# Local attention in 48-query blocks on four 64x64 tiles, global keys in three groups, and part of q and k transposed by DMA

## The chip, the cores and the metric

The kernel runs on one core of a Trainium2 chip. The metric is the device time of one execution in microseconds (us). Runs of the kernel before took 363.45, 364.85 and 365.05 us; the median is 364.85.

The engines are named as the profile names them: PE is TensorE's matmul stream and PEld its weight loads, DVE is VectorE, ACT is ScalarE, POOL is GpSimd, SP is SyncE, which here only issues transfers. A trailing q (SPq) is an engine's queue of instructions.

## The reference, cut to what matters

An attention layer (8 batches, 8 heads, 576 tokens, 64 numbers per head) is followed by an expert layer of two matrix products with ELU between them. The attention is the sum of two softmax attentions: a local one, in which a query sees the keys less than 4 tokens away, and a global one over means of four consecutive tokens (144 queries, 144 keys), whose output is repeated four times.

```python
q_d = q.reshape(B, H, Sd, factor, D).mean(axis=3)      # factor = 4, Sd = 144
k_d = k.reshape(B, H, Sd, factor, D).mean(axis=3)
v_d = v.reshape(B, H, Sd, factor, D).mean(axis=3)
out_d = sm_attn(q_d, k_d, v_d)
out_up = np.repeat(out_d, factor, axis=2)
mask = np.abs(pos[:, None] - pos[None, :]) < factor
scores = np.where(mask, scale * np.matmul(q, k.transpose(0, 1, 3, 2)), -1e9)
out_local = np.matmul(softmax(scores), v)
x = (out_up + out_local)                               # to 4608 tokens x 512
h = x @ w_in                                           # 512 x 2048
g = np.where(h > 0.0, h, np.exp(np.minimum(h, 0.0)) - 1.0)
return g @ w_out                                       # 2048 x 512
```

## The kernel before

**The unit of attention** is a pair of heads of one batch: head e = 0 lies on partitions 0 to 63 and head e = 1 on 64 to 127 once q and k are turned (transposed so that the 64 numbers of a head run along the partitions). There are 4 pairs in each of 8 batches, 32 in all. The steps of a pair are:

- `load` (L433 on): SP loads q and k of the pair as float32, 96 partitions x 768 numbers. In batches 0 and 1 (`SIX`) a partition holds six consecutive tokens (rows of 1536 bytes, L442); in the others a partition takes one token from each of six blocks of 96 tokens (rows of 256 bytes, L444).
- `cast` (L507 on): GpSimd (VectorE for q of batch 0) casts them to float16 tiles `c16`, L516.
- `transposes`: TensorE multiplies the cast tile by a constant. From batch 2 on there are six matmuls per tensor, whose 120 columns are a 96x96 identity and 24 columns that take the means of four (`ONE`, L548). In batches 0 and 1 there are twelve: six with an identity (L536) and six with `BY6`, which takes the means from the layout of six tokens per partition (L540). ACT (VectorE for k of batch 0) evicts the results into `qt`, `kt` and `KD` (L563 to L577).
- `scores`: twelve matmuls of 96 queries against 102 keys (L620), and four of 144 pooled queries against 102 rows of pooled keys (L628), in two groups `kg`. The contraction is over 64 numbers, so the two heads of a pair use the upper and the lower half of the array. Two exponentials on ACT (L637), one for each head, and one multiplication by the band mask on VectorE (L644) follow.
- `denominators`, once per batch (twice for batch 0): 72 small matmuls with indicator columns (L665) collect the sums of the exponentials of four pairs in one bank, VectorE takes the reciprocals (L692, 144 columns). From batch 2 on they are spread over the partitions by a transfer to DRAM and back (`rd`, `rcb`, L719 and L724); in batches 0 and 1 (`BY_PE`) by matmuls with `SEL` (L707) and an eviction (L714).
- `pool_v`: pooled v of a batch, 6 matmuls of 512 columns (L591), in the same TensorE operation as the denominators from batch 1 on; two evictions (L604).
- `outputs`: 12 matmuls with v (L748) and 8 with pooled v (L756) per pair, the two heads side by side in the columns of the array. `normalize` multiplies by the reciprocals on VectorE (L771), then adds the repeated global part to the local one on GpSimd (some of batch 0 on VectorE, L787), into `xt`.

v is loaded by SP as blocks of 96 tokens with their neighbours, 112 rows (L470), and cast by GpSimd (L473).

**The expert layer** works on 9 blocks of 512 tokens. `mm1` makes 16 groups of 4 matmuls of 128x512 per block (L804); ACT takes the exponential (L810), VectorE a minimum and a sum (L812) and the combination into `gt` (L815). `mm2` makes 16 groups of 4 matmuls per block (L827), ACT evicts `os` (L842) and SP stores it (L845). That is 1152 matmuls of 512 columns.

**The order of everything** is made by `Plan.run` when the program is built. It is a list scheduler: each operation has an engine, a planned duration, a rank (its due time, worked out from `PARAM`) and buffers from small pools (`SLOTS`). At each moment an engine takes the operation of the lowest rank whose inputs and buffers are there in the planner's own time; the order that comes out is fixed in the program. On the chip each engine, and each queue of transfers, goes through its list in order and waits where an input is late. `fill` (L329) puts matmuls on zeros between the real ones at the beginning. All loads of q, k and v and all stores of the result are issued by SP, so they stand in one queue in the planned order.

Of the kernel before, what the change touches and what calls it, by code (L numbers as in the profile page):

```python
# [18 lines left out]
NB, QB = 6, 96  # L19
KW = QB + 6  # L20
VB = 112
HB = 3 * QB
HD = SD // 2
GW = HB + HD
# [5 lines left out]
SIX = (0, 1)  # L30
EARLY = 1
DEN_GROUPS = {0: ((0, 1), (2, 3))}
# [4 lines left out]
BY_PE = (0, 1)  # L37
# [4 lines left out]
def _np_sel():  # L42
    sel = np.zeros((NPAIR, 32, 5, 2, 64), dtype=np.float16)
    for e in range(2):
        for i in range(5):
            sel[:, 5 * e + i, i, e] = 1.0
    return sel.reshape(128, 640)
# [22 lines left out]
class Plan:  # L70
# [24 lines left out]
    PARTS = ("v16", "v32", "rcb", "xt", "gt", "ex")  # L95
# [158 lines left out]
    def emit(self):  # L254
        for o in self.order:
# [4 lines left out]
    "ld": 8, "c16": 4, "v16": 2, "v32": 1, "qt": 3, "kt": 3, "ex": 8, "vd": 2,  # L260
# [3 lines left out]
PARAM = dict(M0=30, P=36.77, LAG=1.06, LEAD=53.49, GAP=7.69, SC=3.9, DEN=33.04, OUT=1.4, OUTG=1.98,  # L264
             LOAD=23.14, VLOAD=27.91, VCAST=36.99, warm=3.4, FILL=27.63, WI=-27.58, WO=38.12, WOG=2.24,
             OVER=1.0, LEAD1=57.82, GAP1=5.57, OUT1=32, VLOAD1=41.43, LOAD1=28.31, CC=-45.43, tv0=-26.96,
             C0=-7.99, SC0=2.71, OUTA=-25.9, OUTB=-21.42, DEN0=3.42, DENB=-28.86, SPA=-26.1, SPB=-20.87,
             V0=-46.5, G0=1, G1=2, G2=3, G3=3, G4=3, G5=8, G6=3, G7=13, G8=13, L0=2, L1=6, L2=0, L3=8,
             L4=0, LAG0=1.07, QG=2.08)
# [3 lines left out]
def kernel(  # L273
# [15 lines left out]
    def many(kind, shape, dt=FP16):  # L289
        return [sb.tile(shape, dt, tag=f"{kind}{i}", name=f"{kind}_{i}") for i in range(SLOTS[kind])]  # L290

    T = {
        "ld": many("ld", [QB, 2, NB, 64], FP32),
        "c16": many("c16", [QB, NB, 2, 64]),
        "v16": many("v16", [KW, NPAIR, 2, NB, 64]),
        "v32": many("v32", [115, 48, 64], FP32),
        "qt": many("qt", [128, 720]),
        "kt": many("kt", [128, S + 6]),
        "ex": many("ex", [KW, 2, 2, HB + SD]),
        "vd": many("vd", [QB, 2, NPAIR, 128]),  # L300
        "rcb": many("rcb", [128, NPAIR, 2, GW]),
        "rc": many("rc", [128, SD]),
        "xn": many("xn", [128, 2, GW]),
        "xt": many("xt", [128, DMC, TBLK]),
        "gt": many("gt", [128, FCN, TBLK]),
        "e": many("e", [128, TBLK]),
# [622 lines left out]
```

## Time and profile before

| what | value |
|---|---|
| runs of the kernel | 363.45, 364.85, 365.05 us |
| span of the profiled execution | 362.9 us, granted TensorE clock 0.984 |
| first matmul of the expert layer (L804) | at 37.56 us |
| matmuls of the expert layer | 576 (L804) and 576 (L827) |
| matmuls that transpose, batches 2 to 7 (L548) | 288 |
| ACT: exponentials of the scores (L637) | 64, mean 887 ns |
| VectorE: mask (L644) | 32, mean 895 ns |
| VectorE: minimum (L812) | 144, mean 386 ns |
| GpSimd: casts of q and k (L516) | 60, mean 861 ns |
| transfers on SP's and ACT's hardware queues | 108038 packets, 39.49 MB |
| a load of q, 288 KB, from issue to landing | 5.2 us (median) |

The profile is of one execution, whose span runs from its first to its last instruction. Matmuls are pipelined: the duration of one holds its way through the array, and the distance between the starts of two tells what one costs. In a timeline row stand the start in us, the time that the row's instructions cover, the engine, the source line, the operation, the tiles written and read, the shapes (for a matmul rows*columns of its weights, then partitions x columns of what streams through), the count, and in brackets the idle time of the engine before it with what ended it. In a list of waits stand who waited for whom, the sum in us, how often, and the longest.

### The profile page before, as it was taken

Reading aid. Unit: us, or ns where it says so; the run is one execution under the profiler, and the core shown is the slowest. Engines: PE = TensorE matmul, PEld = TensorE weight load, DVE = VectorE, ACT = ScalarE, POOL = GpSimd, SP = SyncE. Lnnn points to the kernel's source line nnn. Section 1 sums busy time; section 2 is a strip of 40 time slices with the busy share of each in tenths; the row PEclk is TensorE's granted clock in tenths of the full one; section 3 lists DMA queues with packets and bytes.
Section 4 is the critical chain, followed back from the end, with each engine's and each line's share of the span. In section 5 each row is a group of like instructions: output and inputs, shape, how many; then the busy total and the mean of one; then the engine's idle time right before and its main releaser. Section 6 shows DMA issues by size and latency. Waiting matters only on the chain.

```text
span 362.9 us, 8968 instructions
## 1 busy us (share of the span) xinstructions
PE 347.5 (96%) x3677; PEld 189.3 (52%) x3677; DVE 224.4 (62%) x410; ACT 211.5 (58%) x364; POOL 144.0 (40%) x226
## 2 busy tenths in 40 slices
PE   8995999999998998999999999999999999999995
PEld 7984554455454554554555455555554444444442
DVE  3658598336885597557755865398547667765510
ACT  2643696469865677557855785488557415544411
POOL 7645554277274544570557055634330160000000
PEclk9998799899999999999999999999999999999999
DMA  8999999999979799479746975103001311010021
GB/s 218 216 157 225 258 199 191 202 201 235 234 168 222 193 181 220 93 157 214 155 94 153 218 149 99 61 35 83 31 30 60 87 48 40 0 58 33 29 77 68
DMA packets 114366, 48.89 MB, mean 135 GB/s; under 512 B 100662, under 2 KB 108662, under 8 KB 114326
## 3 DMA queue, kind: packets, MB, share of 16 engines
q1 hardware_dynamic: 108038, 39.49, 52.3%
q0 software_dynamic: 6288, 8.84, 13.3%
q8 instruction: 28, 0.46, 0.6%
q14 instruction: 12, 0.10, 0.1%
HBM read 42.86 MB, written 9.66 MB: 145 GB/s over the span
## 4 chain that ended last, share of the span: by engine, by line
PE 78%; DVE 9%; ACT 6%; issue 2%; DMA 2%; POOL 2%; ACTq 0%; DVEq 0%; POOLq 0%
PE bank L827 32%; PE bank L804 27%; PE bank L548 4%; PE bank L620 3%; PE bank L748 3%; DVE e L812 3%; PE bank L329 3%; ACT e L810 2%; DVE gt L815 2%; PE bank L665 2%; ACT ex L637 2%; DVE ex L644 2%; DMA rcb<-rd 1%; PE bank L540 1%; PE bank L756 1%
## 5 line engine op out<-in xcount | busy, mean ns | idle before, releaser
L804 PE MATMUL bank<-xt,WI 128*128 128x512 f16 x576 | 141.2, 382 | 1.6 <-DVE gt L815 1.4
L827 PE MATMUL bank<-WO,gt 128*128 128x512 f16 x576 | 140.3, 381 | 1.9 <-DVE gt L815 1.9
L810 ACT ACTIVATE e<-bank 128x512 f16<-128x512 f32 x144 | 85.1, 603 | 49.1 <-PE bank L804 27.2
L815 DVE SCALAR_TENSOR_TENSOR gt<-bank,e 128x512 f16<-128x512 f32 x144 | 97.8, 688 | 4.9
L827 PEld LDWEIGHTS <-gt 128*128 128x128 f16 x576 | 54.0, 98 | 64.4 <-DVE gt L815 2.6
L804 PEld LDWEIGHTS <-WI 128*128 128x128 f16 x576 | 53.1, 98 | 64.0 <-issue 6.3
L812 DVE TENSOR_SCALAR e<-e 128x512 f16<-128x512 f16 x144 | 55.4, 386 | 39.6 <-ACT e L810 38.8
L516 POOL CAST c<-ld 96x768 f16<-96x768 f32 x60 | 50.6, 861 | 50.5 <-issue 25.7
L637 ACT ACTIVATE ex<-bank 102x864 f16<-102x864 f32 x64 | 53.4, 887 | 23.7 <-PE bank L628 23.5
L787 POOL TENSOR_TENSOR xt<-xn 128x288 f16<-128x288 f16 (+8 forms) x92 | 44.4, 514 | 54.1 <-DVE xn L771 54.0
L644 DVE TENSOR_TENSOR ex<-ex,MASK 102x1152 f16<-102x1152 f16 x32 | 28.6, 895 | 41.5 <-ACT ex L637 41.4
L842 ACT COPY os<-bank 128x512 f32<-128x512 f32 x36 | 21.3, 590 | 46.4 <-PE bank L827 43.4
L771 DVE TENSOR_TENSOR xn<-bank,rcb 128x720 f16<-128x720 f32 x32 | 27.8, 901 | 25.6 <-PE bank L756 23.8
L473 POOL CAST v<-v 102x768 f16<-102x768 f32 x32 | 27.5, 887 | 0.3 <-DMA v<-in_v_dram 0.3
L548 PEld LDWEIGHTS <-c 96*128 96x128 f16 x288 | 18.1, 97 | 8.0 <-issue 0.4
L563 ACT CAST qt<-bank 128x720 f16<-128x720 f32 x24 | 18.3, 761 | 4.2 <-PE bank L548 3.7
L548 PE MATMUL bank<-ONE,c 96*128 96x120 f16 x288 | 20.6, 216 | 0.0
L719 POOL DMA_DIRECT2D rd<-rc x6 | 3.5, 578 | 41.3 <-DVE rc L692 19.7
L329 PE MATMUL bank<-zero 128*128 128x128 f16 x221 | 17.3, 240 | 1.8 <-DVE ONE L355 1.1
L620 PEld LDWEIGHTS <-kt 64*102 64x102 f16 x384 | 11.7, 125 | 12.6 <-ACT e L810 4.7
L575 ACT CAST kt<-bank 128x576 f16<-128x576 f32 x24 | 15.6, 651 | 1.2 <-ACT qt L563 1.2
L329 PEld LDWEIGHTS <-zero 128*128 128x128 f16 x221 | 15.1, 109 | 2.4 <-DVE zero L332 1.1
(67 smaller groups left out, 228.6 us busy)
## 6 DMA issues: line engine op xcount, KB each, us to landing
ld<-in_q_dram SPq DMA_DIRECT2D x32, 288.0 KB, 5.2
ld<-in_k_dram SPq DMA_DIRECT2D x32, 288.0 KB, 5.4
out_dram<-os SPq DMA_DIRECT2D x36, 256.0 KB, 2.0
v<-in_v_dram SPq DMA_DIRECT2D x13, 672.0 KB, 8.8
rcb<-rd POOLq DMA_DIRECT2D x12, 360.0 KB, 5.6
WO<-in_moe_w_out_dram POOLq DMA_DIRECT2D x4, 512.0 KB, 9.1
WI<-in_moe_w_in_dram POOLq DMA_DIRECT2D x3, 512.0 KB, 11.3
v<-in_v_dram SPq DMA_DIRECT2D x3, 336.0 KB, 8.6
```

The source lines that it names most:

```text
L329: nc.tensor.matmul(PS[:, 7, 384:512], zero[:, 0:128], zero[:, 128:256], start=True, stop=True)
L516: f(out=at(y)[:], in_=at(x)[:].rearrange("p e c d -> p c e d"))
L548: nc.tensor.matmul(o, t[:, c, :, :], C["ONE"][:], start=True, stop=True)
L637: lambda e=e: nc.scalar.activation(out=at(x)[:, e], in_=two(sc[e], 0, KW, 0, HB + SD), func=AF.Exp, scale=SCALE),
L644: nc.vector.tensor_tensor(out=a, in0=a, in1=mk, op=AB.mult)
L771: lambda: nc.vector.tensor_tensor(out=at(w)[:], in0=two(z, 0, 128, 0, GW), in1=at(y)[:, j], op=AB.mult),
L787: (nc.vector if eng == "DVE" else nc.gpsimd).tensor_tensor(out=at(xt(t))[:, j, o : o + n - a], in0=ln, in1=gn, op=AB.add)
L804: nc.tensor.matmul(one(h, 0, 128, 0, TBLK), WI[:, dc, 128 * fc : 128 * fc + 128], at(x)[:, dc, :], start=(dc == 0), stop=(dc == DMC - 1),)
L810: op("ACT", 0.55, r, lambda: nc.scalar.activation(out=at(e)[:], in_=one(h, 0, 128, 0, TBLK), func=AF.Exp), reads=[h], writes=[e], name=f"e ...
L812: op("DVE", 0.42, r, lambda: nc.vector.tensor_scalar(out=at(e)[:], in0=at(e)[:], scalar1=1.0, scalar2=-1.0, op0=AB.min, op1=AB.add), reads ...
L815: op("DVE", 0.64, r, lambda: nc.vector.scalar_tensor_tensor(out=at(gt)[:, fc, :], in0=one(h, 0, 128, 0, TBLK), scalar=0.0, op0=AB.max, in1 ...
L827: nc.tensor.matmul(one(z, 0, 128, 0, DM), at(gt)[:, fc, 128 * tt : 128 * tt + 128], WO[:, fc, :], start=(fc == 0), stop=(fc == FCN - 1),)
```

## The change

The local attention goes from 6 blocks of 96 queries and 102 keys to 12 blocks of 48 queries and 54 keys, on 64 partitions each. Even and odd blocks lie on the lower and upper 64 partitions of the scores, so a score matmul uses 64 rows (one head) and 64 columns (one parity) of the array, and four of these tiles fill it. The pooled keys come in three groups of 64 rows instead of two of 102. The tiles that hold exponentials, v and pooled v change accordingly, and the means are indexed in ten groups of 72 columns instead of five of 144 (`IND`, `GAP`, `SEL`).

All loads of q and k now use rows of six tokens. Two ways of turning them remain: `transposed` is the form that batches 0 and 1 had (twelve matmuls per tensor), and `turned` is a transfer that transposes the cast tile from SBUF to SBUF, issued by SP. `TURNED` picks q of batches 3 to 7 (`TQ` = 12 pairs in) and k of batches 4 to 7 (`TK` = 16): 36 of 64 tensors. Tensors of batch 2, and k of batch 3, that had six matmuls now have twelve. For turned tensors GpSimd forms the sums of four tokens in two steps (`pa`, one addition; `pb`, three), VectorE scales them (`pc`), and ACT copies a turned k into its padded layout (`kn`).

v is loaded in two halves of 64 partitions, each with its own transfer, and pooled v takes 24 matmuls of 256 columns in two operations of their own. The two exponentials per pair become one over 128 partitions, the mask covers half as many columns, the reciprocal 72 columns instead of 144. The multiplication in `normalize` is split in two instructions. `PARAM` holds other ranks throughout, so the planned order of all engines differs.

```diff
-SIX = (0, 1)
+NS, QB = 6, 48
+KB = 64
+LW = NS * QB
 SLOTS = {
-    "ld": 8, "c16": 4, "v16": 2, "v32": 1, "qt": 3, "kt": 3, "ex": 8, "vd": 2,
+    "ld": 8, "c16": 4, "sg": 3, "ex": 6, "v16": 2, "v32": 1, "ps": 1, "vd": 2,
...
+    TURNED = {(b, j, w) for b in range(2, B) for j in range(NPAIR) for w in "qk"
+              if NPAIR * b + j >= PARAM["TQ" if w == "q" else "TK"]}
...
-                if b in SIX:
-                    nc.sync.dma_start(out=t.rearrange("p e c d -> p e (c d)"), in_=sixes(src, b, j))
-                else:
-                    nc.sync.dma_start(out=t, in_=rows(src, b, j, 0, QB, 0, NB))
+                nc.sync.dma_start(out=at(x)[:].rearrange("p e c d -> p e (c d)"), in_=sixes(src, b, j))
...
-            nc.sync.dma_start(out=t[0:VB, c0:c1, :], in_=blocks(c0, c1, -3, VB))
+            nc.sync.dma_start(out=t[p : p + KB, c0:c1, :], in_=blocks(h, c0, c1, 0, KB))
...
+    def turned(b, j, i, y, w, r):
+        r += PARAM["TU"]
+        o = op("SP", 1.25, r + 0.1 * i,
+               lambda: nc.sync.dma_start_transpose(out=at(w)[:, i], in_=at(y)[:].rearrange("p c e d -> p (c e d)")),
+               reads=[y], writes=[w], nbytes=S * 256, rate=112e3, packet=36, name=f"tu{'qk'[i]}{b}{j}")
+
+        def natural():
+            nc.scalar.copy(out=KN[w.slot[0]][:, KOFF : KOFF + S], in_=at(w)[:, 1].rearrange("p c u -> p u c"))
+
+        if i:
+            op("ACT", 0.65, r + PARAM["KN"], natural, writes=[w], after=[o_fill, o], name=f"kn{b}{j}")
+
+    def pooled(b, j, dma, w, r):
+        u, a, n = Buf("ps"), dma[0], len(dma)
+
+        def first():
+            t = at(w)[:, a : a + n].rearrange("p w (c x) u -> p w c x u", x=2)
+            nc.gpsimd.tensor_tensor(out=at(u)[:, a : a + n], in0=t[:, :, :, 0], in1=t[:, :, :, 1], op=AB.add)
+
+        op("POOL", 0.15 + 0.5 * n, r + 1.0, first, after=[x for x in w.writers if x.name[:2] == "tu"], writes=[w, u], name=f"pa{b}{j}")
+
+        def second():
+            x = at(u)[:, a : a + n].rearrange("p w c (g u x) -> p w c g u x", g=6, x=2)
+            o = PD[w.slot[0]][:, a : a + n].rearrange("p w (g u) -> p w g u", g=6)
+            for m, (c0, x0, c1, x1) in enumerate(((0, 0, 1, 0), (2, 0, 0, 1), (1, 1, 2, 1))):
+                nc.gpsimd.tensor_tensor(out=o[:, :, :, m:24:3], in0=x[:, :, c0, :, :, x0], in1=x[:, :, c1, :, :, x1], op=AB.add)
+
+        o = op("POOL", 0.4 + 0.25 * n, r + 1.1, second, reads=[u], writes=[w], after=[o_fill], name=f"pb{b}{j}")
+
+        def scale():
+            t = PD[w.slot[0]][:, dma[-1]]
+            nc.vector.tensor_scalar_mul(out=t, in0=t, scalar1=1.0 / (16.0 if n == 2 else 4.0))
+
+        op("DVE", 0.13, r + 1.2, scale, writes=[w], after=[o], name=f"pc{b}{j}")
...
-            for g in range(2):
-                for i in range(3):
+            for s in range(3):
+                for x in range(4):
                     nc.tensor.matmul(
-                        PS[32 * i : 32 * i + 32, z.slot[0] + g, :], C["VR"][:], t[:, :, :, 3 * g + i, :],
-                        start=True, stop=True, tile_position=(0, 32 * i),
+                        PS[32 * x : 32 * x + 32, zs[g].slot[0] + s // 2, 256 * (s % 2) : 256 * (s % 2) + 256],
+                        C["VR"][:], t[:, 2 * g : 2 * g + 2, :, 2 * s + x % 2, :],
+                        start=True, stop=True, tile_position=(0, 32 * x),
                     )
...
-            for c in range(NB):
+            for c in range(2 * NS):
                 for e in range(2):
                     p = slice(64 * e, 64 * e + 64)
-                    qa = QB * c if m else 120 * c
                     nc.tensor.matmul(
-                        PS[0:KW, sc[e].slot[0] + c // 3, QB * (c % 3) : QB * (c % 3) + QB],
-                        kt[p, QB * c : QB * c + KW], qt[p, qa : qa + QB], start=True, stop=True,
+                        PS[64 * (c % 2) : 64 * (c % 2) + KB, z.slot[0] + e, QB * (c // 2) : QB * (c // 2) + QB],
+                        kn[p, QB * c : QB * c + KB], qt[p, :, 8 * c : 8 * c + 8].rearrange("p c u -> p u c"),
+                        start=True, stop=True,
                     )
+            for i in range(3):
+                for h in range(2):
+                    for e in range(2):
+                        p = slice(64 * e, 64 * e + 64)
+                        nc.tensor.matmul(
+                            PS[64 * h : 64 * h + 64, z.slot[0] + e, LW + GH * i : LW + GH * i + GH],
+                            pd[p, 1, 64 * i : 64 * i + 64], _free(pd[p, 0, 96 * h : 96 * h + 1], [[32, 3], [1, 24]]),
+                            start=True, stop=True,
+                        )
...
-        for e in range(2):
-            op("ACT", 0.84, r + 0.3 + 0.1 * e,
-               lambda e=e: nc.scalar.activation(
-                   out=at(x)[:, e], in_=two(sc[e], 0, KW, 0, HB + SD), func=AF.Exp, scale=SCALE),
-               reads=[sc[e]], writes=[x], name=f"ex{b}{j}{e}")
+        op("ACT", 1.07, r + 0.3, lambda: nc.scalar.activation(
+            out=at(x)[:], in_=two(z, 0, 128, 0, EW), func=AF.Exp, scale=SCALE), reads=[z], writes=[x], name=f"ex{b}{j}")
...
+            for s in range(NS):
+                for h in range(2):
                     for e in range(2):
                         nc.tensor.matmul(
+                            PS[64 * e : 64 * e + 64, z.slot[0] + h, QB * s : QB * s + QB],
+                            v_[64 * h : 64 * h + 64, j, e, s, :], ex[64 * h : 64 * h + 64, e, QB * s : QB * s + QB],
+                            start=True, stop=True,
                         )
+            for i in range(3):
+                for h in range(2):
+                    for e in range(2):
+                        o = 128 * (j % 2) + 64 * e
+                        nc.tensor.matmul(
+                            PS[64 * e : 64 * e + 64, z.slot[0] + h, LW:HW],
+                            d_[64 * h : 64 * h + 64, j // 2, i, o : o + 64],
+                            ex[64 * h : 64 * h + 64, e, LW + GH * i : LW + GH * i + GH],
+                            start=(i == 0), stop=(i == 2),
+                        )
```

Of `PARAM`, the prediction uses `TU` = -0.4 (the rank of a turning transfer) and `SC`, the rank of the scores, 3.9 before and 8.25 after, both counted from the same due time of the pair.

437 lines of the change are left out of this document (195 added, 242 removed).

## The prediction

> **What bounds the kernel now.** I read the page first, then TensorE's timeline over one batch in the middle, then the waits, then the timeline around the places where TensorE stood still.
>
> ```profile
> span 362.9 us, 8968 instructions
> PE 347.5 (96%) x3677; PEld 189.3 (52%) x3677; DVE 224.4 (62%) x410; ACT 211.5 (58%) x364; POOL 144.0 (40%) x226
> ```
>
> TensorE (PE) is busy nearly throughout, the others near half. A busy share says little of pipelined matmuls, so I price TensorE by slots: from the first start of an operation to the first start of the next. These are rows of TensorE's timeline between 132 and 149 us:
>
> ```profile
> 132.44 0.32 PE L665 MATMUL bank<-ex,GAP 96*32 96x72 f16 x16
> 132.57 0.44 PE L665 MATMUL bank<-ex,IND 102*32 102x144 f16 x20
> ...
> 132.96 0.62 PE L591 MATMUL bank<-v,VR 102*32 102x512 f16 x6
> 133.51 1.04 PE L804 MATMUL bank<-xt,WI 128*128 128x512 f16 x4
> ...
> 139.85 0.48 PE L620 MATMUL bank<-qt,kt 64*102 64x96 f16 x12
> 140.17 0.29 PE L628 MATMUL bank<-qt,kd 64*102 64x144 f16 x4
> 140.39 1.90 PE L804 MATMUL bank<-xt,WI 128*128 128x512 f16 x8
> 142.13 0.80 PE L548 MATMUL bank<-ONE,c 96*128 96x120 f16 x12
> 142.76 1.03 PE L804 MATMUL bank<-xt,WI 128*128 128x512 f16 x4
> ...
> 147.82 0.45 PE L748 MATMUL bank<-ex,v 102*64 102x96 f16 x12
> 148.10 0.30 PE L756 MATMUL bank<-ex,vd 96*64 96x72 f16 x8
> 148.24 0.42 PE L748 MATMUL bank<-ex,v 102*64 102x96 f16 x12
> ```
>
> Twelve transposing matmuls (L548) take 142.76 - 142.13 = 0.63 us, 52 ns each. A pair's scores take 0.54 us (139.85 to 140.39), about 0.44 in its 16 matmuls and 0.10 in leaving that array shape. A pair's output takes 0.42 (147.82 to 148.24). The expert layer's matmuls run at 0.216 us each: the page's 576 + 576 make 249 us, and from 291 us on they are nearly alone and nearly gapless. So the end is the sum of TensorE's slots, plus the start (the first L804 is at 37.56 us), plus its stalls. Over 0.216 us each, the dense matmuls lose about 12 us in all; about 5 are changes of shape, 7 are stalls. What makes a stall is seen here (all engines, 99 to 112 us):
>
> ```profile
> 99.82 1.60 POOL L473 CAST v<-v 102x768 f16<-102x768 f32 x2
> 100.19 1.38 DVE L812 TENSOR_SCALAR e<-e 128x512 f16<-128x512 f16 x1 [0.96 <-ACT e L810]
> 102.22 0.28 DVE L812 TENSOR_SCALAR e<-e 128x512 f16<-128x512 f16 x1
> ...
> 104.58 4.35 DVE L644 TENSOR_TENSOR ex<-ex,MASK 102x1152 f16<-102x1152 f16 x1 [0.43 <-ACT ex L637]
> 111.60 0.39 PE L827 MATMUL bank<-WO,gt 128*128 128x512 f16 x1 [1.29 <-DVE gt L815]
> ```
>
> L812 takes 0.28 us alone and 1.38 beside a GpSimd cast; the mask takes 4.35 where its median is 0.76, with GpSimd at work 3.97 us of it; TensorE then waits for VectorE's gt.
>
> **TensorE's part of the change.** *Turning.* A batch from 2 on now spends 48 matmuls at 52 ns, 2.5 us, on transposes. After, batches 4 to 7 spend none (-10.1). Batch 3 keeps k alone in the heavier form of batches 0 and 1 (12 matmuls per tensor; at 8.66 and 9.30 us two such groups follow each other 0.64 apart), so 4 x 0.63 = 2.5, unchanged. Batch 2 keeps q and k in that form, 8 x 0.63 = 5.0 (+2.5). Sum: -7.6 us.
>
> *Scores and outputs.* Each becomes 36 matmuls per pair (24 of 48 columns, 12 of 72) instead of 16 and 20. No row has four tiles split both ways, so the price per matmul is bounded: 16 GAP matmuls, four 32-column tiles at once, take 0.13 us, 8 ns each; the 8 of L756, 64-column weights two at a time, take 0.14 us, 17.5 each. 36 of them are 0.29 to 0.63 us. I take 14 ns, 0.50 us: nearer the L756 row because the weights are again 64 wide, and four tiles move 256 weight columns where GAP's four move 128. That is +0.06 on scores (0.44) and +0.08 on outputs (0.42), over the 28 pairs of batches 1 to 7 (batch 0 lies in the start): +1.7 and +2.2 us. By the bounds the two together range from -7.8 to +11.2.
>
> The Trainium skill speaks against this: TensorE: Matmul & The Clock Gate, Back-to-back issue gap and the floors before it, says that starts never come closer than about 25 ns however few columns. By it 36 matmuls would take 0.90 us and the two parts would cost +26 us instead of +3.9. The 16 GAP matmuls, at 8 ns each, contradict it where several tiles run side by side.
>
> *Denominators, pooled v, spreading.* 72 denominator matmuls become 56 (-0.3 us a batch by the GAP rate), pooled v goes from 6 of 512 columns three at a time (0.55 us) to 24 of 256 four at a time (six groups at half a dense 0.216, 0.65), now as two operations that may add a change of shape of 0.1 each. I take 0, bounds -2 to +2 over seven batches. Batch 1's spreading goes from 6 to 10 matmuls a pair: +0.4.
>
> TensorE in all: -7.6 + 1.7 + 2.2 + 0.4 = **-3.3 us**.
>
> **The other engines.** They set no end of their own but feed the stalls. ACT: two exponentials of 0.887 become one of 1008 columns; from 720, 864 and 576 columns (0.761, 0.887, 0.642) a column costs 0.83 ns, so 1.01: -0.76 x 32 = -24. Evictions of q and k (0.761 + 0.651 + 0.302 a pair, 24 pairs, 41 us) become about 22: eight pairs' worth of mixed evictions (7.5 + 3.7) and 16 copies of k at 0.65. VectorE: the mask halves (-11), reciprocals of 72 columns instead of 144 (-4), 20 small scalings (+3). GpSimd gains: a fp16 add costs 0.18 us + 1.75 ns a column (from 236 ns at 32 and 684 at 288), so the first sum of q and k is 1.19 us and the three second ones 3 x 0.35; for 16 pairs 2.2 each, for 4 pairs with q alone 1.5, **+42 us** on 144. That it stays off the path: in batches 4 to 7 it would be busy some 26 of 36 us. What it costs VectorE: L812 waits in 44 of 144 cases (606 ns mean against 289), the mask in 13 of 32, some 18 us lost for 144 of GpSimd, so 42 more cost 5 us, of which 7/18 reached TensorE: +2. Against that stand 43 us less on ACT and 12 on VectorE. I take stalls -1, bounds -4 to +5.
>
> **The start.** On the chain to the first L804 stand two denominator groups (36 and 25 matmuls shown, about 0.9 us each) and two reciprocals of 1.06; they lose about 1.4. SEL doubles (+160 KB) and v is read as 128 rows instead of 112 (+0.2 MB for batch 0): 0.36 MB at the 207 GB/s of the first 38 us is 1.7 us of transfers, hidden as long as they land before their readers. I take -0.5, bounds -2 to +2.
>
> **Transfers.** 36 transposing transfers, SBUF to SBUF, 144 KB each, are issued by SP between casts and scores. No row shows one. Lower bound of issue and landing: 0.31 and 2.2 us (a 288 KB load's issue; the 36 KB rd transfer's landing); upper: 2.7 and 8.8 (v). The loads of batches 2 to 7 move to 1536-byte rows, which can only relieve the queues. I take the loads' 5.2 us landing and cost it at 0, hidden by the lead that the code gives it: ranks put the transfer 0.4 us before and the scores 8.25 us after the same point.
>
> **Sum:** 362.9 - 3.3 - 0.5 - 1 = 358.1 us of span. The runs' median, 364.85, lies 1.95 over the profiled span, so **360 us**; by itself 354 to 364.
>
> **Rivals.** (1) *Four tiles truly at once.* If loading 256 weight columns costs no more than GAP's 128, scores and outputs fall to 0.30 us: 28 x 2 x 0.20 = 11 us less, 349. For it: the two column tiles of L756 do overlap. Against it: no row loads more than about 4 weight columns per ns (GAP 32/8.1, L756 64/17.5, L620 102/27).
>
> (2) *Slower: the transposing transfers come late.* Between a cast and the scores lie SP's issue (up to 2.7), the landing (2.2 to 8.8), GpSimd's sums (2.2) and up to two casts queued before them (1.7): with 5.2 for the landing 9.5 to 11.8 us, against the 8.65 of lead. SP's queue is in order and is mostly waiting already:
>
> ```profile
> SPq L845 <- ACT os L842: 169.0, 30, 20.1
> ```
>
> A transfer behind such a store can't run ahead, so lateness isn't paid once but at every pair, and TensorE, in order too, waits with all dense matmuls behind the scores. It decides from a landing of about 4 us on if issue and casts also queue; at 0.6 us for each of 20 pairs, +12: 372. Against it: the planned order leaves 8 us between pairs, and buffers for three pairs let a transfer start before it is due. Trainium skill, VectorE: DVE Perf Modes, The three transpose paths, gives 1309 ns for a DMA transpose of 128x128 against 390 on TensorE; six blocks would, by an estimate, take 7.9 us and fall on this rival's side. No run here shows it yet.
>
> (3) *GpSimd eats the gain.* All 5 us that VectorE loses reach TensorE, as after the 4.35 us mask: 365.
>
> **Chances.** The forecast 0.42, (1) 0.13, (2) 0.28, (3) 0.17. Range 350 to 371: it leaves out the far half of (1) and of (2). About 0.5% (1.8 us) is what a measurement here can tell from none: faster holds the forecast but for its upper edge, and (1) and a little of (3), 0.56; same the middle of (3) and that edge, 0.14; slower (2) and the rest of (3), 0.30.
>
> **What would show it.** Turning: no transposing matmuls after batch 3. Scores and outputs: slots of 36 matmuls near 0.50 us plus the shape change (0.3 is (1), 0.9 the floor). Stalls: the mean of the 128x512 minimum (386 ns) rising means (3). Transfers: TensorE waiting before scores for VectorE's scaling or GpSimd's sums means (2), and SP's waits then name the casts or os. The start: the first dense matmul at 37. I am wrong above all if those waits appear at every turned pair.

## The result, and the profile after

The changed kernel's runs took 385.39, 385.82, 393.73 and 402.06 us; the kernel before took 362.94 to 365.05 beside it (median 364.15). The ratio is 1.0595, with a 95% interval of 1.0539 to 1.0651: some 21 us slower, where 360 us had been forecast. Ratios here and below leave out executions over 1.5% above a kernel's fastest (here 393.73 and 402.06 us), but the profiles of e1, e2, e3, e6, e7, f1 and f2 are of such longer ones, so that a single stop in them can be longer than the ratio's runs had it. The profiled execution spans 383.7 us against 362.9. The page after:

```profile
span 383.7 us, 11243 instructions
PE 349.3 (91%) x4749; PEld 189.8 (49%) x4749; DVE 229.6 (60%) x470; ACT 189.0 (49%) x300; POOL 190.1 (50%) x308
...
L814 PE MATMUL bank<-xt,WI 128*128 128x512 f16 x576 | 140.4, 381 | 8.5 <-DVE gt L825 7.1
...
L822 DVE TENSOR_SCALAR e<-e 128x512 f16<-128x512 f16 x144 | 60.8, 423 | 54.9 <-ACT e L820 54.5
...
L551 POOL TENSOR_TENSOR ps<-sg 128x576 f32<-128x576 f16 (+1 forms) x20 | 23.6, 1179 | 1.6 <-DMA sg<-c 1.6
L559 POOL TENSOR_TENSOR pd<-ps 128x96 f16<-128x96 f32 (+1 forms) x60 | 24.2, 436 | 0.3
...
L565 DVE TENSOR_SCALAR pd<-pd 128x192 f16<-128x192 f16 x20 | 13.7, 684 | 11.7 <-POOL pd L559 11.7
```

L814 and L837 are now the expert layer's matmuls, L822 the minimum, L551 and L559 GpSimd's sums, L565 the scaling. GpSimd went from 144 to 190 us, ACT from 212 to 189. The minimum's mean rose from 386 to 423 ns, and the scaling takes 684 ns, where its fastest rows of this shape take 0.20 us. Who waited for whom:

```profile
POOL rcb L728 <- DMA rd<-rc: 13.6, 4, 5.0
...
DVE pd L565 <- POOL pd L559: 11.7, 8, 3.9
...
PE bank L814 <- DVE gt L825: 7.1, 9, 2.9
...
PE bank L639 <- DVE xn L783: 6.6, 2, 4.8
DVE xn L779 <- DMA rcb<-rd: 6.6, 5, 2.7
```

Priced by slots (from start to start) from the first dense matmul on, as in the prediction, the 20.8 us divide so. Dense are the expert layer's matmuls of 512 columns; a wait counts to the slot that it lengthens, so a wait in front of a pair's scores lies in the dense matmuls:

| part of TensorE's time | before, us | after, us |
|---|---|---|
| start, to the first dense matmul | 37.4 | 39.4 |
| dense matmuls over 0.216 us each, waits behind them included | 13.3 | 31.0 |
| scores, waits inside a pair's matmuls included | 15.7 | 24.7 |
| turning | 19.0 | 13.8 |
| outputs | 13.4 | 11.8 |
| denominators, pooled v, spreading | 11.6 | 10.7 |

The dense matmuls, which the change does not touch, lost 17.7 us; scores 9.0, 4.8 of it waits inside the 28 trains (a train is the row of small matmuls of one pair; 0.71 us each without a wait). Turning, outputs and the small parts gained 7.7. TensorE's long stops end at 157.7 us (4.8 us), 195.8 (3.3), 200.4 (1.9), 231.4 (2.9) and 261.9 (1.7); in the kernel before no two starts between 50 and 300 us lie 2 us apart. Two kinds are among them. The first, all engines, 148 to 159 us:

```profile
148.21 1.24 POOL L728 DMA_DIRECT2D rcb<-rd  x2 [5.04 <-DMA rd<-rc]
149.46 1.28 POOL L551 TENSOR_TENSOR ps<-sg 128x576 f32<-128x576 f16 x1
...
151.46 1.20 POOL L559 TENSOR_TENSOR pd<-ps 128x96 f16<-128x96 f32 x3
...
152.70 0.79 DVE L565 TENSOR_SCALAR pd<-pd 128x192 f16<-128x192 f16 x1 [3.91 <-POOL pd L559]
...
156.68 0.76 DVE L779 TENSOR_TENSOR xn<-bank,rcb 128x576 f16<-128x576 f32 x1 [1.33 <-DMA rcb<-rd]
...
158.68 1.01 ACT L656 ACTIVATE ex<-bank 128x1008 f16<-128x1008 f32 x1 [8.57 <-PE bank L648]
```

GpSimd stands 5.04 us for the landing of its own write rd before it may issue rcb (rd landed 1.8 to 4.3 us after its issue in the kernel before, 5.3 to 6.2 in batches 2 to 5 here); the sums are queued behind, VectorE stands 3.91 us at the scaling for them, and the normalisation xn (L779), late for rcb, holds the PSUM banks that the next scores need. The second kind, 226 to 232 us:

```profile
227.27 1.22 POOL L559 TENSOR_TENSOR pd<-ps 128x96 f16<-128x96 f32 x3
227.32 3.31 DVE L822 TENSOR_SCALAR e<-e 128x512 f16<-128x512 f16 x1 [0.95 <-ACT e L820]
...
228.42 0.83 POOL L519 CAST c<-ld 96x768 f16<-96x768 f32 x1
229.20 1.27 POOL L551 TENSOR_TENSOR ps<-sg 128x576 f32<-128x576 f16 x1
...
231.41 1.50 PE L814 MATMUL bank<-xt,WI 128*128 128x512 f16 x4 [2.90 <-DVE gt L825]
```

Here nobody waits for a result: a minimum of 0.28 us takes 3.31 while GpSimd works without a gap until 230.47, and it ends 0.16 us after that. That the one is the cause of the other is what the later runs test.

### The profile page after: what moved, and what is told of

Same layout as the page of the kernel before. It is cut to its first block, busy times and chain, and to the rows that moved or that the text cites. A ratio compares the mean times of both kernels' runs of the same rounds, so it can differ in the third digit from the quotient of the medians.

```text
span 383.7 us, 11243 instructions
## 1 busy us (share of the span) xinstructions
PE 349.3 (91%) x4749; PEld 189.8 (49%) x4749; DVE 229.6 (60%) x470; ACT 189.0 (49%) x300; POOL 190.1 (50%) x308
## 4 chain that ended last, share of the span: by engine, by line
PE 70%; DMA 10%; DVE 8%; POOL 5%; issue 3%; ACT 2%; SPq 1%; DVEq 0%; ACTq 0%; POOLq 0%
PE bank L837 26%; PE bank L814 26%; DMA rcb<-rd 7%; PE bank L639 4%; PE bank L334 3%; DVE e L822 3%; PE bank L580 3%; DMA v<-in_v_dram 2%; PE bank L577 2%; PE bank L753 2%; DVE gt L825 2%; POOL xt L797 1%; PE bank L613 1%; DMA out_dram<-os 1%; ACT e L820 1%
## 5 line engine op out<-in xcount | busy, mean ns | idle before, releaser
L814 PE MATMUL bank<-xt,WI 128*128 128x512 f16 x576 | 140.4, 381 | 8.5 <-DVE gt L825 7.1
L837 PE MATMUL bank<-WO,gt 128*128 128x512 f16 x576 | 140.9, 388 | 3.5 <-DVE gt L825 3.3
L825 DVE SCALAR_TENSOR_TENSOR gt<-bank,e 128x512 f16<-128x512 f32 x144 | 98.8, 689 | 5.3
L822 DVE TENSOR_SCALAR e<-e 128x512 f16<-128x512 f16 x144 | 60.8, 423 | 54.9 <-ACT e L820 54.5
L837 PEld LDWEIGHTS <-gt 128*128 128x128 f16 x576 | 55.2, 99 | 70.2 <-issue 9.1
L814 PEld LDWEIGHTS <-WI 128*128 128x128 f16 x576 | 53.7, 98 | 72.0 <-issue 12.0
L656 ACT ACTIVATE ex<-bank 128x1008 f16<-128x1008 f32 x32 | 32.2, 1012 | 48.0 <-PE bank L648 38.5
L779 DVE TENSOR_TENSOR xn<-bank,rcb 128x576 f16<-128x576 f32 x32 | 24.0, 750 | 24.6 <-PE bank L762 13.2
L661 DVE TENSOR_TENSOR ex<-ex,MASK 128x576 f16<-128x576 f16 x32 | 19.0, 594 | 32.0 <-ACT ex L656 31.9
L473 POOL CAST v<-v 128x768 f16<-128x768 f32 x32 | 26.8, 866 | 21.5 <-DMA v<-in_v_dram 21.5
L639 PE MATMUL bank<-sg,kn 64*64 64x48 f16 x768 | 21.9, 256 | 6.8 <-DVE xn L783 6.6
L551 POOL TENSOR_TENSOR ps<-sg 128x576 f32<-128x576 f16 (+1 forms) x20 | 23.6, 1179 | 1.6 <-DMA sg<-c 1.6
L559 POOL TENSOR_TENSOR pd<-ps 128x96 f16<-128x96 f32 (+1 forms) x60 | 24.2, 436 | 0.3
L639 PEld LDWEIGHTS <-kn 64*64 64x64 f16 x768 | 15.3, 118 | 17.1 <-issue 14.6
L580 PE MATMUL bank<-BY,c 96*128 96x144 f16 x168 | 19.6, 232 | 2.6 <-issue 1.5
L565 DVE TENSOR_SCALAR pd<-pd 128x192 f16<-128x192 f16 x20 | 13.7, 684 | 11.7 <-POOL pd L559 11.7
## 6 DMA issues: line engine op xcount, KB each, us to landing
WO<-in_moe_w_out_dram POOLq DMA_DIRECT2D x4, 512.0 KB, 11.6
```

The costliest lines, as they stand in the source:

```text
L473: nc.gpsimd.tensor_copy(out=at(x)[:, j].rearrange("p e c d -> p (e c) d"), in_=at(x32)[:, 12 * j : 12 * j + 12, :])
L580: nc.tensor.matmul(PS[:, z.slot[0] + 1, LW : LW + SD], t[:, c, :, :], C["BY6"][:, c], start=(c == 0), stop=(c == NR - 1),)
L639: nc.tensor.matmul(PS[64 * (c % 2) : 64 * (c % 2) + KB, z.slot[0] + e, QB * (c // 2) : QB * (c // 2) + QB], kn[p, QB * c : QB * c + KB], q ...
L656: op("ACT", 1.07, r + 0.3, lambda: nc.scalar.activation(out=at(x)[:], in_=two(z, 0, 128, 0, EW), func=AF.Exp, scale=SCALE), reads=[z], wri ...
L814: nc.tensor.matmul(one(h, 0, 128, 0, TBLK), WI[:, dc, 128 * fc : 128 * fc + 128], at(x)[:, dc, :], start=(dc == 0), stop=(dc == DMC - 1),)
L822: op("DVE", 0.42, r, lambda: nc.vector.tensor_scalar(out=at(e)[:], in0=at(e)[:], scalar1=1.0, scalar2=-1.0, op0=AB.min, op1=AB.add), reads ...
```

## The experiments

Each kernel is the changed kernel with one edit, unless it says otherwise. Ratios are to the kernel before on the same chip, with 95% intervals.

**First theory: the reciprocals' trip through DRAM, which has no slack in the new order, and the rivals from the prediction.**

```
 xn:  in1=rcb   ->   in1=FIX (a constant tile)          # e1
 tu:  dma_start_transpose   ->   dma_start, 1152-byte rows    # e2
```

> The changed kernel in its own order, but in batches 2 to 7 the attention output is multiplied by a constant tile in place of the reciprocals that come back from DRAM, so nothing waits for their landing (the transfers still run; the normalisation is left out). Theory A (the spread reciprocals land late): the stalls of 5.0 and 5.5 us at 148 and 190 us, the 1.8 us of slower matmuls after each, and the smaller ones at the same place in batches 2, 5 and 6 go; span 383.7 falls to 366 to 371. Rival B (TensorE's own slots, scores above all, carry the loss) and rival C (GpSimd's sums block VectorE): 380 to 384, the gaps only move to another wait.

Measured 1.0545 [1.0494, 1.0597], 383 us: 3 us gained at most, though xn waits for no transfer. In its profile VectorE still stood 5.0 us for the sums, and one mask took 5.84 us where its median is 0.46. The trip alone is not it.

> The changed kernel in its own order, but the 36 transposing transfers are plain copies of as many bytes from SBUF to SBUF (1152-byte rows in place of 576 pieces of 256 bytes each; the transposing is left out, so q and k of the later batches are not turned). If the transposing transfers are what stretches the reciprocals' trip from 11 us (recip to landing, before) to 15 us, the trip falls to 11 to 12 us in batches 3 to 5 and the span to 370 to 376. If the loads of v are what it queues behind, the trip stays at 14 to 16 us and the span at 381 to 385.

Measured 1.0588 [1.0539, 1.0638], as the changed kernel. That the transfers transpose costs nothing that shows.

```
 qt[p, :, 8*c : 8*c+8].rearrange("p c u -> p u c")   ->   qt[p, :, 8*c : 8*c+8]     # e3
 TQ=12, TK=16   ->   TQ=32, TK=32                                                  # e4
```

In e3 mask and xn follow the new order of columns.

> The changed kernel with the 48 query columns of a score block streamed as six runs of 8 neighbours in place of 48 columns 96 apart; the band mask and the multiplication by the reciprocals are put in the same order, so the result is the reference's. If the step of the streamed columns is what makes a group of four score tiles take 84 ns where the output's take 32, the 24 matmuls fall from 0.50 to 0.20 us, a pair's slot from 0.71 to about 0.42, and the time by up to 8 us, less what the waits for the reciprocals take back: 375 to 381. If the weight loads of four tiles are the limit, the slot stays at 0.71 and the time within 2 us.

Measured 1.0532 [1.0478, 1.0586], 381 to 384 us, between what the two cases expected. These are rows of TensorE's timeline for a pair's scores and two pairs' outputs, first of the changed kernel, then the scores of e3:

```profile
185.57 0.68 PE L639 MATMUL bank<-sg,kn 64*64 64x48 f16 x24
186.07 0.28 PE L648 MATMUL bank<-pd 64*64 64x72 f16 x12
186.28 1.04 PE L814 MATMUL bank<-xt,WI 128*128 128x512 f16 x4
...
189.84 0.38 PE L753 MATMUL bank<-ex,v 64*64 64x48 f16 x24
...
190.57 1.04 PE L814 MATMUL bank<-xt,WI 128*128 128x512 f16 x4
```

```profile
189.84 0.38 PE L639 MATMUL bank<-sg,kn 64*64 64x48 f16 x24
190.05 0.27 PE L648 MATMUL bank<-pd 64*64 64x72 f16 x12
190.26 1.04 PE L815 MATMUL bank<-xt,WI 128*128 128x512 f16 x4
```

With query columns 96 elements apart 24 score matmuls take 0.50 us, in runs of eight 0.21; the train falls from 0.71 to 0.42 us. Over 32 trains that is 9 us of TensorE's time, of which the kernel gave back some 2: it mostly waits instead.

> The changed kernel with no tensor turned by a transfer: all 64 by TensorE in the form of twelve matmuls; no sums on GpSimd, no scaling, no copy of k on ACT; the planned order follows. TensorE gains 36 x 0.63 = 22.7 us of matmuls. Theory A with the transfers as its cause: the stalls go, 372 to 378, so turning by transfer is worth nothing here. If the stalls have nothing to do with turning: 383.7 + 22.7, 400 to 408.

Measured 1.0635 [1.0602, 1.0668], 386 us, in the range of neither case. Without the transfers and what follows them the dense matmuls' excess is back at 13.3 us, and TensorE's turning, in the heavy form, takes 37.0 instead of 13.8. So the 23 us that the transfers save against this form are lost again by what comes with them; since the planned order follows the edit, this is no clean comparison.

**Second theory: the queues of GpSimd and VectorE, part by part.**

```
 pc on VectorE (L565)   ->   nc.gpsimd.tensor_scalar_mul, behind pb       # e5
 pa, pb, pc             ->   left out, same order                        # e6
 rcb reads rd of b      ->   rd of b - 1 (rd in two buffers by turns)    # e7
 BY_PE = (0, 1)         ->   BY_PE = tuple(range(8))                     # e8
```

> The 20 scalings of the pooled q and k move from VectorE to GpSimd, behind the sums there: VectorE no longer waits for GpSimd's sums (11.7 us in 8 waits in the changed kernel). What is computed stays. Theory D (VectorE stands at the scaling with min and elu of the expert layer queued behind it): the stops of TensorE near 148, 190 and 225 us go, some 10 to 15 us with the slow matmuls behind them; 370 to 376 us. Rival E (the loss is GpSimd's own lateness: it gives pooled keys and landed reciprocals late whoever scales): no more than 3 us gained, 382 to 387 us, and the wait shows at the global scores (line 648) instead.

Measured 1.0705 [1.0647, 1.0763], 388 to 392 us: worse than either expectation (370 to 376, 382 to 387). VectorE's waits for the sums are gone, but the same stops lead back to the trip, and single minima take 3.1 to 3.4 us.

> The sums on GpSimd and the scaling on VectorE are left out, in the same order of the rest (pooled q and k of the turned pairs are zeros or what stood there, so the global scores are wrong); the transposing transfers and the eviction of k stay. Theory D: 28 us of GpSimd and the 13.7 us of scalings go, and with them most of the 17.8 us that the dense matmuls lose above 0.216 us each; 362 to 372 us. Rival E (the lateness comes with the reciprocals' trip through DRAM and the transfers, not with the sums): 378 to 386 us.

Measured 1.0459 [1.0411, 1.0507], 381 us, in rival E's range. The chain of waits in e6's profile (an execution of 390.43 us), 148 to 166 us:

```profile
148.45 5.60 DMA rd<-rc
...
154.33 0.45 POOL rcb L728
...
154.95 9.71 DMA rcb<-rd
...
165.45 0.31 DVE xn L783
...
165.80 0.70 PE bank L639 x24
```

With no sums at all, the trip through GpSimd's queue holds scores in the same place.

> The spreading transfers of batches 3 to 7 read the DRAM rows that the batch before wrote (two buffers in turn; the outputs are divided by another batch's denominators), so GpSimd does not stand 4 to 6 us waiting for the landing of its own write; the order is the same. Theory D (that wait holds the sums behind it): GpSimd's 13.6 us of waits at line 728 go, VectorE's waits at the scaling fall from 11.7 us to under 4, 370 to 377 us. Rival E (the sums themselves are late, 1.3 us each behind casts and adds): the scaling's waits stay near 10 us, 381 to 386 us.

Its runs lie between 384.69 and 400.31 us, too far apart for a verdict, and none is near 377. In the profile (400.31 us) GpSimd no longer stands for its write, and one scaling on VectorE takes 13.58 us (its median is 0.42), within 0.1 us of the end of a gapless run of GpSimd.

> TensorE spreads the reciprocals of all eight batches, as it does for the first two: no trip through DRAM, 18 transfers fewer on GpSimd's queue, 24 trains of ten small matmuls more on TensorE (0.18 us each, 4.3 us) and 24 evictions on ScalarE (0.71 us each, 17 us). What is computed stays. Theory D: the trip's 15 us and GpSimd's standing go, 4.3 us are paid: 368 to 376 us. Rival E (sums and transfers alone are the cause): 384 to 391 us.

Measured 1.0639 [1.0590, 1.0688], 388 us, in rival E's range. No trip is left, and this is what stands in its place, all engines, 164 to 177 us:

```profile
165.32 11.12 DVE L661 TENSOR_TENSOR ex<-ex,MASK 128x576 f16<-128x576 f16 x1 [1.90 <-ACT ex L656]
165.34 2.36 POOL L473 CAST v<-v 128x768 f16<-128x768 f32 x3
...
172.17 1.27 POOL L551 TENSOR_TENSOR ps<-sg 128x576 f32<-128x576 f16 x1
...
174.17 1.21 POOL L559 TENSOR_TENSOR pd<-ps 128x96 f16<-128x96 f32 x3
175.31 0.83 POOL L519 CAST c<-ld 96x768 f16<-96x768 f32 x1
176.37 0.28 DVE L822 TENSOR_SCALAR e<-e 128x512 f16<-128x512 f16 x1
```

A mask of 0.46 us stands through eleven microseconds of GpSimd's casts, adds and sums and ends 0.3 us after the last. TensorE stops for 7.9 us behind it, to 177.4 us.

So it looks as if each edit takes one loss away and uncovers the other: a GpSimd that waits is late, and a GpSimd that no longer waits runs on and holds VectorE. The next run makes both edits.

**Third theory (T): both go together.**

```
 f1:  e6 + e7, same order                  g5:  f1 + pa, pb written to a scratch tile, no pc
 f2:  pa, pb on VectorE + e8               g2:  f1 + e3
```

> Both edits at once, in the order of the changed kernel: no sums and no scalings (global scores wrong), and the spreading transfers read the rows of the batch before (outputs divided by another batch's denominators), so that GpSimd neither carries the 28 us of sums nor stands for its own write. Theory T (each edit alone only trades one loss for the other: a GpSimd that waits is late with what stands behind it, and a GpSimd that runs without a gap holds VectorE's mask, min and scaling, 11.1 us at one mask in e8 and 13.6 us at one scaling in e7; both go only together): 362 to 370 us, no stop of VectorE over 3 us. Rival Q (the loads and transposing transfers on SP's queue are late whatever GpSimd does): 378 to 386 us, TensorE's stops near 150 and 195 us remain and lead back to SP's transfers.

Measured 1.0102 [1.0065, 1.0140], 368 us: 18 us back, where e6 alone gave 4 or 5 and the fastest run of e7 (384.69) one. No operation of VectorE stands over 1.5 us, and the dense matmuls' excess is 15.6 us. Rival Q, SP's queue, falls: its transfers are all there.

> The sums of the turned pairs move to VectorE (fp16), beside the scaling there, and TensorE spreads the reciprocals of all batches; what is computed stays. GpSimd loses 28 us of sums and 18 transfers, TensorE gains 9 us of small matmuls (as in e8), VectorE some 20 us. Theory T: against e8's 386 us the 11 us stop at the mask goes and no trip is waited for: 368 to 376 us. Rival Q: 382 to 388 us.

Measured 1.0342 [1.0304, 1.0379], 377 us, 11 under e8 and 9 under the changed kernel, computing the same (the first sum in fp16), at the upper edge of what T expected. The stop at the mask is gone; TensorE pays 9 us of spreading.

> f1_prev_no_sums with the sums put back on GpSimd, in the order of the changed kernel, but written to a scratch tile that nothing reads, and no scalings (f1's outputs). Between f1 (368 us, no sums) and e7 (385 to 400 us, sums that VectorE waits for). Theory T (the sums' GpSimd time, with the port that it holds, is the price): 378 to 392 us, one stop of VectorE's mask or min over 4 us. Rival W (the price is VectorE's wait for the sums before it scales): 366 to 372 us.

Measured 1.0711 [1.0632, 1.0789], 389 us, against 368 without the sums. This is the sharpest of the runs: the sums are read by nobody, VectorE waits for none of them, GpSimd waits for nothing of the trip, and 21 us are gone. All engines, 162 to 176 us:

```profile
166.54 1.27 POOL L552 TENSOR_TENSOR ps<-sg 128x576 f32<-128x576 f16 x1
166.91 7.86 DVE L662 TENSOR_TENSOR ex<-ex,MASK 128x576 f16<-128x576 f16 x1 [5.99 <-ACT ex L657]
...
173.25 1.21 POOL L560 TENSOR_TENSOR XPD<-ps 128x96 f16<-128x96 f32 x3
174.69 0.28 DVE L823 TENSOR_SCALAR e<-e 128x512 f16<-128x512 f16 x1
...
175.75 2.72 PE L815 MATMUL bank<-xt,WI 128*128 128x512 f16 x6 [4.68 <-DVE gt L826]
```

The mask stands 7.86 us and another at 212.6 us 4.52, a minimum at 231.2 us 3.30; behind each TensorE stands, 4.7 us until 175.7, 3.1 until 218.1 and 2.9 until 235.3. A rival would be that GpSimd's own products come late. The pages, first of f1, then of g5, tell what TensorE waited for before its first product:

```profile
L814 PE MATMUL bank<-xt,WI 128*128 128x512 f16 x576 | 139.8, 381 | 4.1 <-DVE gt L825 3.0
...
L815 PE MATMUL bank<-xt,WI 128*128 128x512 f16 x576 | 143.5, 388 | 17.2 <-DVE gt L826 16.4
```

The waits for VectorE's gt rose by 13.4 us, and the dense matmuls' excess from 15.6 to some 35; TensorE's waits for GpSimd's casts stayed at 1.0. So the price comes through VectorE, and rival W falls.

> f1_prev_no_sums with the query columns of the scores streamed as six runs of eight, as in e3 (outputs as wrong as in f1). In e3 a train of scores fell from 0.711 to 0.414 us, 9.5 us over 32 trains, and the kernel gained 2 us, because it waited on. Theory T (with the queues' losses gone TensorE's time counts): 358 to 362 us, 6 to 10 us under f1. Rival V (something else holds f1 too): 364 to 369 us.

Measured 0.9932 [0.9885, 0.9980]: 0.017 under f1, some 6 us, where the same edit gave 2 in e3. Over all ten runs, 358.7 to 366.5 us, the median is 364.2, above the expected 358 to 362 and 3.6 us under f1's 367.8. So the gain is some 4 to 6 us, and whether g2 is faster than the kernel before (median 364.5 beside it) is open.

**On the kernel before.** Added to it, at the place where the scores are issued:

```
+        for b > 2:  pa, pb of after's shapes, GpSimd, scratch tiles
 g1:  after=[o_fill]          g4:  after=[o_fill, *casts of the pair]
```

> The kernel before, with the sums of the changed kernel added to GpSimd on scratch tiles for the 20 pairs of batches 3 to 7 (same shapes, same number, some 40 us of GpSimd); nothing reads what they write, so no engine waits for them, and the outputs are those of before. Theory T (GpSimd's time itself is the price: it delays casts, adds and transfers queued behind, and while it runs without a gap VectorE's mask and min stand): 4 to 12 us slower, 367 to 376 us, VectorE's excess over its usual durations rises from 22 us by 8 us or more. Rival U (only work that another engine waits for costs time): within 2 us of before, 362 to 366 us.

> As g1_before_more_gpsimd (382 us, with the added sums packed into the first 150 us), but each pair's sums can only follow that pair's casts, as in the changed kernel, so that the 40 us or so of GpSimd lie between 90 and 280 us. Still nothing reads them. Theory T: GpSimd's gapless stretches in batches 3 to 7 grow, VectorE stands there, 366 to 376 us. Rival U (before has slack there, and g1's loss was one of the crowded first batches): 362 to 366 us.

g1 measured 1.0473 [1.0424, 1.0523], 382 us, and g4 1.0222 [1.0164, 1.0279], 372 us, with the outputs of the kernel before. GpSimd's time alone costs 8 to 17 us; in g1 it fell into the first 115 us, with one stretch of 40 us without a gap. From the pages of before and of g4:

```profile
L804 PE MATMUL bank<-xt,WI 128*128 128x512 f16 x576 | 141.2, 382 | 1.6 <-DVE gt L815 1.4
...
L823 PE MATMUL bank<-xt,WI 128*128 128x512 f16 x576 | 142.2, 382 | 8.9 <-DVE gt L834 8.9
```

VectorE's time over the median of each of its shapes rose from 21 to some 34 us in both. In g1 another 3.8 us is one wait for a load of WO, which stands in GpSimd's queue, so not all of its price comes through VectorE. Rival U falls; g1 lies above T's own span.

**Can the tiles be had without the loss?** Three kernels keep the four tiles and turn as before does, from natural rows, with scores on columns in a row: f3 all tensors, f4 all but 14, g3 all but 4, each in an order planned anew; turned tensors are summed on VectorE.

```
 b > 1, not TURNED:  load natural rows; 6 matmuls, ONE [96, 120]; q, k evicted in natural order
 f3: TQ=32, TK=32     f4: TQ=20, TK=30     g3: TQ=30, TK=30
```

> The new attention (four 64x64 tiles, 48-query blocks, global keys in 3 groups) with the turning of the kernel before: natural rows are loaded, six 120-column matmuls turn and average each tensor of batches 2 to 7, q is kept in natural order so that scores stream columns in a row; no transposing transfers, no sums, no scalings; the planned order has 0.3 to 6.8 us between the landing of the reciprocals and the first outputs. Theory T: turning 19 us as before, scores 13 us, outputs 12, the excess of the dense matmuls 13 as before: about 5 us less TensorE time than before and a start 2 us later; 357 to 363 us, at or under before. Rival R (four tiles and 48-query blocks cost more elsewhere than they save): 366 to 374 us.

> As f3_old_turning, with q from pair 20 and k from pair 30 on (14 tensors) turned by transposing transfers, evicted to natural order by ScalarE, and summed by VectorE. Each turned tensor saves 0.315 us of TensorE, 4.4 us together; ScalarE and VectorE take 16 and 10 us more. Theory T (turning by transfers is worth its TensorE time once GpSimd's queue has no part in it): 2 to 5 us under f3. Rival Q (the transfers delay SP's loads): as f3 or up to 5 us above.

> As f4_some_turned, with q turned by transfers from pair 30 on alone and k from pair 30 on (4 tensors), planned with the durations that f4's profile shows for ScalarE and VectorE instead of the shorter ones. What is computed stays. If f3 and f4 lost their gain over before to an order planned with durations that were too short (their stops at 113, 140 and 159 us): 358 to 363 us, at or under before. Rival R (the tiles themselves cost elsewhere): 367 to 373 us.

f3 measured 1.0250 [1.0220, 1.0281], 373 us, and g3 1.0117 [1.0039, 1.0196], 367.5 us (median), both in the range of rival R, over before. f4 measured 1.0174 [1.0087, 1.0262], which lies between two pairs of runs (366.17 and 367.63, 372.90 and 374.62 us), so a gain on f3 by turning some tensors with transfers is not shown.

In f3's profile scores (12.7 us) and outputs (12.7) are under before's 15.7 and 13.4, but the first dense matmul comes at 42.6 us, 5 late, and turning takes 23.4 instead of 19.0, waits included. In g3's profile the first dense matmul comes at 45.8 us, 8.5 late, and the rest of the span takes 319.4 us, where it takes 325.5 before. So g3 is in R's range for another reason than R's: it loses at the start, while scores (14.9 us) and outputs (12.3) are again under before's. No version that computes the reference beat the kernel before. Whether the tiles would with a start as early as before's is open.

## Why the prediction was wrong, point by point

**The step that failed** is the other engines': "L812 waits in 44 of 144 cases (606 ns mean against 289), the mask in 13 of 32, some 18 us lost for 144 of GpSimd, so 42 more cost 5 us, of which 7/18 reached TensorE: +2", netted to stalls of -1 with bounds -4 to +5. The mechanism had been seen, in the 4.35 us mask (with GpSimd at work 3.73 us of it, not 3.97), and rival (3) carried it; its size was wrong. The 44 and 13 are those that met GpSimd at all; longer than alone were 25 minima and 4 masks, and the one mask of 4.35 us made most of what the masks lost. So the loss lay in few long stops even before, and a share of GpSimd's busy time could not price it. The dense matmuls' stalls grew by 17.7 us. The sign named for rival (3), the mean of the minimum, rose by only 37 ns, 5 us in all: a few long stops carry the loss, not the mean. g5 against f1 measures the sums at 21 us, g4 and g1 the same load on the kernel before at 8 and 17. The price does not follow GpSimd's busy time, as the rule of three had it; what grew much more is its stretches without a gap. Joined from the starts and ends of GpSimd's rows in each trace between 90 and 290 us (a pause of up to 0.08 us counted as none):

| kernel | longest stretch, us | in stretches over 5 us, us | ratio to before |
|---|---|---|---|
| before | 10.4 | 33.6 | 1 |
| f1 | 9.1 | 47.0 | 1.0102 |
| g4 | 19.4 | 85.4 | 1.0222 |
| e8 | 18.8 | 94.4 | 1.0639 |
| changed kernel | 20.8 | 112.8 | 1.0595 |
| g5 | 20.1 | 119.2 | 1.0711 |
| g1 | 23.7 | 57.3 | 1.0473 |
| e6 | 9.5 | 43.9 | 1.0459 |
| e4 | 6.2 | 47.6 | 1.0635 |

A third more work made three times as much of it gapless. The order is not strict, since it also matters which operation falls into a stretch, and the last three rows show that stretches are not the only loss: g1 has one of 40.1 us ahead of 90 us; e6 waits for the trip, and e4 turns everything on TensorE.

**The cover by ACT and VectorE** ("43 us less on ACT and 12 on VectorE"). ACT's busy time fell by 23 us (the copy of k takes 1.18 us, not 0.65), VectorE's rose by 5 where 12 less had been forecast, so the cover did not come about.

**Moved past a queue.** The sums were costed as work, not as something that stands behind GpSimd's wait for its write rd. That wait is worth little while the sums are there (as far as e7's runs tell) and about 13 us once they are gone (e6 to f1, 1.0459 to 1.0102). In the kernel before, the outputs' normalisation began 0.6 to 5.8 us after rcb had landed in batches 2 to 6 (0.1 in batch 7); after, 0.1 to 0.3 us in all six. The prediction had no term for that slack.

**Rival (2), late transposing transfers**, was right that the kernel would be slower and wrong about why: plain copies (e2) are as slow, the transfers landed 4.2 us after issue (median) where 5.2 had been taken, TensorE waited 3.4 us in all for the scaling before the global scores, and f1 keeps every transfer and is at 1.0102.

**Scores and outputs.** Both were priced at 0.50 us for 36 matmuls. Outputs take 0.37 (10 ns each): the four tiles do overlap, nearly as in rival (1). The Trainium skill, TensorE: Matmul & The Clock Gate, Wait — 56ns, not 53.3ns?, has starts never closer than about 25 ns; these rows, like the 8 ns of the denominators, go under it where four tiles work at once. Scores take 0.71, because the query columns lie 96 elements apart, which the prediction did not price; in runs of eight 0.42. g2 against f1 puts this at 4 to 6 us of time.

**Turning** was forecast at -7.6 and came to -5.2, waits in it included; the small parts at +0.4 and came to -0.9; the start at -0.5 and came to +2.0. The 20 scalings were priced at 3 us and took 13.7, again beside GpSimd (the plan has 0.13 us for one, which took 0.68).

**What the forecast amounts to without the failed step.** g2, which lacks the sums, GpSimd's wait and the strided columns, is at 0.9932 [0.9885, 0.9980]; over all its runs it is level with the kernel before, and the forecast was 360/364.85 = 0.987. TensorE's sum was about right: without the 4.8 us of waits in the scores the table gives -3.5 us, and -3.3 was forecast. That is luck in part, since scores came 2.5 and turning 2.4 us over their terms, outputs 3.8 and the small parts 1.3 under. What was wrong by far is the queues.

## What to carry to other kernels

Work given to an idle engine is not free when that engine shares something with a busy one: before adding GpSimd work, look how long its stretches without a gap become and which VectorE operations with all operands in SBUF fall into them, and price a stretch, not a sum. When two waits cover each other, taking one away shows nothing; take both, then put one back. And where a small matmul streams columns far apart, price the step of the columns too.

## What the runs showed of the hardware

An operation of VectorE on SBUF alone (mask, minimum, scaling) that comes up while GpSimd works without a gap can stand to the end of the whole stretch: 3.31, 7.86, 11.12 and 13.58 us, each over within 0.06 to 0.32 us of GpSimd's last instruction. Operations that also read PSUM do not: L825 takes 689 ns after and 688 (L815) before. The Trainium skill, SBUF — State Buffer, Who interferes with whom, has the two engines share a port pair under an exclusive lock, so that the second to come blocks for the whole instruction of the first, and leaves out an operation with at most one input in SBUF that runs outside its two-port modes. The trace agrees, and goes further: in these four cases the one that waits does not get its turn between two instructions of GpSimd that follow each other directly. Not always: a minimum of the changed kernel ended after 1.94 us, at 135.92 us, in the middle of a stretch from 124.9 to 137.9 us.

After a stop of 5 us TensorE's dense matmuls ran at half speed for a while: 8 of them took 3.53 us from 158.59 us on, 0.44 each instead of 0.216, and the granted clock from 158 to 163 us was 0.50.

The profiles' first dense matmul lay between 36.3 and 46.8 us. In e6, e7 and f2 it came at 46.1 to 46.8 us; there the granted clock from 22 to 28 us was 0.50, where the changed kernel (39.4 us) had 1.00, and in e6 and f2 the same row of 26 filling matmuls took 2.77 us instead of 1.45. That is a part of the delay; why the clock was lower, and where the rest comes from, stays open. So does why rd lands later in the changed kernel, and why rcb takes up to 9.7 us to land in e6 (median 7.1) where the median before is 5.6 and the longest 9.0.
